# A pooled-attention and gated-MLP kernel: the second batch's attention product head by head in whole fp32 numbers

## The chip, the core and the metric

The kernel runs on one core of one Trainium2 chip. The metric is the device time of one execution in microseconds (us). Before the change the median of three runs is 535.81 us (535.55 to 536.28).

Names used below: PE is the matrix engine (PEld its weight loads, which have a row of their own in the trace), DVE the vector engine, ACT the scalar engine, POOL the general engine, SP the engine that only issues DMAs. PSUM is the memory that PE writes to, SBUF the working memory of all engines.

## What is computed

Eight batches, eight heads, 576 positions, head size 64. Keys and values are averaged over groups of 8 positions (so 72 pooled positions), softmax attention runs against them, the heads are laid side by side (512 columns), and a gated MLP with a mixing matrix over positions follows.

```python
k_p = k.reshape(B, H, 72, 8, D).mean(axis=3);  v_p = v.reshape(B, H, 72, 8, D).mean(axis=3)
scores = q @ k_p^T / sqrt(D);  e = exp(scores - max);  attn = e / (sum(e) + 1e-9)
x = (attn @ v_p), heads side by side                       # [8, 576, 512]
h = gelu(x @ w_in);  u, v = h[..., :512], h[..., 512:]
v_n = (v - mean) / sqrt(var + 1e-6) * g_ln
gated = u * (einsum('ts,bsd->btd', w_sg, v_n) + b_sg)
out = x + gated @ w_out
```

## The kernel before

All arithmetic must hold fp32 accuracy. Most matrix products therefore work on numbers split into a high and a low part in the format fp32r: for x = hi + lo and w = hi + lo the kernel issues three products (hi·hi, hi·lo, lo·hi). A product of whole fp32 numbers is one instruction in the program, and in the trace it stands as two matmuls, each with its own weight load.

The work is cut into steps, named by a letter, an index and a batch: `V1+2` is step V, index 1, batch 2. One list, `ORDER`, written out as a table of such names, says in which order the steps (each a generator that yields between its parts) are issued. All engines work through their instructions strictly in that order, so the table sets both what PE does next and what stands ahead of what on DVE, ACT, POOL and SP. A second table, `OTHER`, says for many small operations (copies, casts, subtractions) which of two engines does them.

The steps that the change and the prediction touch:

- D: filler matmuls on an identity matrix, 2 of whole fp32 numbers each; the program has 12 such steps.
- A, B, C, E: loads of keys, values, queries and of the values' last rows ("left"); `lv0`, `v1` and the like load and split the weights `w_in`, `w_sg`, `w_out`.
- K, S: pooled keys; scores of a pair of heads (a "group", 4 per batch), 5 fp32 matmuls with 144 columns each, then maximum, exponential, sum, the guard 1e-9, reciprocal and the product into `e`.
- P: pooled values. From batch 1 on, P2 puts the two heads of each group block by block into a 128 x 128 matrix, split into `vbh` and `vbl`. A group has 2 x 72 = 144 pooled rows, 16 more than the array has rows, so the 16 left over go into a second matrix `vl`.
- T: `e` is turned by 32 x 32 transposes on DVE and a trip through DRAM (`tfar`), loaded as `al` and split into `ah` (cast on ACT) and `al` (difference on DVE). L does the same for the 16 left-over rows of all groups (`lfar`, `lt`).
- V: the attention product. For each half of 288 positions it is four fp32r matmuls into the same 128 PSUM rows: `vbh·ah`, `vbl·ah`, `vl·lt`, `vbh·al`. The result x is copied and split (`x32`, `xhl`).
- H (and J for batch 0), U, W, O, Z: the MLP. H4 works on the last 64 positions and has matmuls with 64 weight columns between such with 128. O multiplies the gated values `ghi`, `glo` by `w_out`; Z stores.

Batch 0 takes another way through V: two products of whole fp32 numbers for each half (`vb·ah`, `vl·lt`), both over all 128 columns. `aps` and `mps` are the two pairs of PSUM tiles: attention uses the first, the MLP the second.

Of the kernel before, what the change touches and what calls it, by code (L numbers as in the profile page):

```python
# [31 lines left out]
V2+0 u1 u0 u0 s3 ls1 V0+0 s2 s0 J1+0 u2 u2 u2 T3+0 V3+0 V2+0 V2+0 u3 s4 s4 u2 A1+1 u3 o0 J1+0 K1+1 V3+0 o0 K1+1 J2+0
H0+0 lo1 B0+1 V3+0 B1+1 u3 u3 K0+1 s0 P0+1 s2 J2+0 J3+0 J3+0 H1+0 H0+0 o1 o0 V1+0 C2+1 V3+0 H0+0 V2+0 H2+0 D0+0 H1+0
H3+0 H2+0 S0+1 o0 o2 H0+0 H4+0 H1+0 H1+0 H1+0 C1+1 S1+1 S0+1 H0+0 H1+0 o1 H0+0 H3+0 S1+1 S1+1 S2+1 H4+0 S0+1 S2+1
S2+1 o2 U0+0 U0+0 H4+0 H4+0 s1 o1 o1 H2+0 S3+1 H2+0 o2 P1+1 U1+0 U2+0 H3+0 A0+2 U1+0 S0+1 o3 H4+0 H2+0 A1+2 K0+2 o3
H3+0 C0+2 U2+0 o2 T0+1 S0+1 H4+0 H2+0 S3+1 H3+0 T0+1 H4+0 H3+0 H4+0 U3+0 C3+2 o3 B0+2 S1+1 S1+1 S2+1 K0+2 S2+1 U3+0
o3 C1+2 W0+0 W1+0 W0+0 S3+1 S3+1 S3+1 S0+2 L0+1 T1+1 W0+0 W0+0 T0+1 L0+1 S0+2 P2+1 W1+0 P2+1 P2+1 P2+1 K1+2 W2+0
T0+1 S1+2 S0+2 L0+1 W2+0 S0+2 W1+0 W3+0 L0+1 V0+1 W3+0 C2+2 W2+0 T1+1 W1+0 T2+1 W3+0 W2+0 O0+0 V0+1 S0+2 K1+2 S1+2
O1+0 T1+1 T1+1 V1+1 S1+2 W3+0 B1+2 S1+2 L0+1 S2+2 V1+1 O0+0 O1+0 T2+1 V1+1 C0+3 P0+2 T2+1 T3+1 O0+0 S2+2 O2+0 T2+1
O1+0 E0+2 V2+1 T3+1 S2+2 T0+2 A0+3 O2+0 V1+1 V0+1 O2+0 Z2+0 T1+2 S2+2 V2+1 V2+1 O3+0 V0+1 O3+0 S2+2 T3+1 S3+2 T3+1  # L40
V3+1 S1+2 C1+3 O3+0 Z3+0 S3+2 V3+1 V3+1 K0+3 S3+2 H0+1 B0+3 V3+1 T0+2 H0+1 S3+2 H1+1 H0+1 H1+1 K0+3 S3+2 H2+1 H2+1
H0+1 H0+1 L0+2 H1+1 H1+1 H0+1 H3+1 H3+1 S0+3 H1+1 H3+1 T0+2 V2+1 H4+1 U0+1 H1+1 P1+2 H4+1 C0+4 P2+2 P2+2 H2+1 L0+2
L0+2 H4+1 U0+1 L0+2 P2+2 P2+2 U1+1 U1+1 S1+3 U2+1 H4+1 P2+2 S0+3 H2+1 H4+1 H2+1 L0+2 Z1+0 Z0+0 A1+3 H3+1 H3+1 H2+1
T0+2 V0+2 U3+1 K1+3 P0+3 H3+1 U2+1 H4+1 H4+1 U3+1 T1+2 C2+3 T2+2 S0+3 T3+2 H4+1 S1+3 W0+1 W0+1 K1+3 W1+1 T1+2 T1+2
V0+2 V1+2 W0+1 S0+3 W1+1 W1+1 W1+1 B1+3 T2+2 V1+2 S1+3 S1+3 V1+2 T2+2 S2+3 S2+3 T2+2 W2+1 W3+1 C3+3 V2+2 T3+2 W2+1
W2+1 S3+3 W2+1 W0+1 O0+1 V0+2 A0+4 T0+3 W3+1 W3+1 W3+1 O1+1 V2+2 C1+4 T1+3 V2+2 O0+1 E0+3 T3+2 T3+2 S2+3 V3+2 O0+1
# [36 lines left out]
""".split()


OTHER = set("""
G10 G11 G12 G13 H00 H10 H12 H13 H21 H22 H23 V00 V01 V02 V03 V13 V21 V22 V23 V33 W01 W10 W13 W21 W22 W23 X00 X03 X21
X22 X23 X30 X31 X32 X33 c10 c11 c21 e00 e01 e10 e11 e12 e20 e21 e22 e30 e31 e32 e33 g00 g04 g10 g11 g22 g24 h00 h02
h20 k10 k11 k20 k21 k31 l2 m00 m02 m03 m10 m11 m12 m21 m23 m30 m31 m32 m33 n00 n02 n03 n10 n11 n20 n21 n23 n30 n31
n32 n33 o0d o0h o1h o2d o3h p10 p11 p21 p30 s2 s2d s3 s3d s4d u0d u1d u2d u2h u3d u3h v0h v1h v2d v2h v3d x00 x01  # L90
x02 x22 z10 z20 z21 z30 z32 z33 z34
""".split())
# [765 lines left out]
```

## Time and profile before

| | before |
|---|---|
| median of the runs | 535.81 us (535.55 to 536.28) |
| profiled execution | 535.39 us, of which span 533.6 us |
| PE busy | 526.6 us, 99%, 3600 matmuls |
| weight loads busy | 498.8 us, 93% |
| DVE / ACT / POOL busy | 391.0 / 273.9 / 247.3 us (73 / 51 / 46%) |
| granted PE clock | 1.0 of full speed in every slice |
| chain that ended last | 94% PE |

How to read it: matmuls overlap in the record (one is entered with some 295 ns while the next begins 132 ns later), so what a matmul costs is read from the distance between starts, not from its own duration. A block of matmuls stands in the timeline as one row with its start, its length up to the end of the last one, and its count. "Idle before" a row is the time in which the engine had nothing running, with the instruction that released it.

### The profile page before, as it was taken

To read this page: it belongs to the slowest core of one execution; us is meant where nothing else is said; L and a number is where in the kernel's file an instruction comes from. 1 tells how busy PE (TensorE), PEld (TensorE's weight loads), DVE (VectorE), ACT (ScalarE), POOL (GpSimd) and SP (SyncE) were. 2 spreads that over 40 slices of the span, in tenths; PEclk is the share of its full clock that TensorE was granted. 3 is DMA by queue.
4 is the path that set the end of the run, shared out by engine and by line. 5 is a ranking of instruction groups with operands and counts; after the bars stand their busy time and mean duration, and the time that the engine had idled before them with its cause. 6 is when DMAs were issued, how large, how long until landed. Compare 5 with 4: busy or idle time off the path is not lost.

```text
span 533.6 us, 9547 instructions
## 1 busy us (share of the span) xinstructions
PE 526.6 (99%) x3600; PEld 498.8 (93%) x3600; DVE 391.0 (73%) x599; ACT 273.9 (51%) x521; POOL 247.3 (46%) x347
## 2 busy tenths in 40 slices
...
GB/s 282 398 332 172 68 146 117 192 208 112 135 139 155 154 114 201 71 109 157 91 152 78 60 174 180 88 58 166 106 137 3 83 117 68 23 1 1 90 1 89
DMA packets 42654, 67.08 MB, mean 126 GB/s; under 512 B 5232, under 2 KB 21616, under 8 KB 42608
## 3 DMA queue, kind: packets, MB, share of 16 engines
...
q10 hardware_dynamic: 288, 0.44, 0.2%
...
## 4 chain that ended last, share of the span: by engine, by line
PE 94%; DVE 2%; ACT 2%; POOL 1%; issue 0%; SPq 0%; DMA 0%; ACTq 0%; POOLq 0%
PE mps L140 79%; PE aps L140 15%; PE aps L186 1%; DVE nmax L506 1%; SPq L240 0%; DMA y<-lfar 0%; DVE glo L230 0%; POOL e L458 0%; ACT lt L559 0%; ACT raw L284 0%; POOL rstd L482 0%; ACT vg L662 0%; DVE e L463 0%; DVE mps L716 0%; ACT vg L491 0%
## 5 line engine op out<-in xcount | busy, mean ns | idle before, releaser
L140 PE MATMUL mps<-xhl,wih 128*128 128x288 f32 x512 | 88.8, 295 | 0.2 <-ACT vg L662 0.2
L140 PE MATMUL mps<-wih,xhl 128*128 128x512 f32 x256 | 81.2, 397 | 0.0
L140 PEld LDWEIGHTS mps<-xhl,wih 128*128 128x128 f32 x512 | 75.1, 188 | 1.0 <-ACT vg L662 0.4
L458 POOL TENSOR_TENSOR e<-e,ssum 128x720 f32<-128x720 f32 x28 | 41.4, 1481 | 62.6 <-DVE ssum L457 55.5
L140 PEld LDWEIGHTS mps<-wih,xhl 128*128 128x128 f32 x256 | 48.0, 188 | 10.9
L140 PE MATMUL mps<-wsh,vhh 128*128 128x288 f32 x256 | 55.2, 297 | 0.0
L140 PE MATMUL mps<-wsl,vhh 128*128 128x288 f32 x256 | 54.7, 295 | 0.0
L140 PE MATMUL mps<-wsh,vhl 128*128 128x288 f32 x256 | 54.6, 294 | 0.0
L140 PE MATMUL mps<-xhl,wil 128*128 128x288 f32 x256 | 54.5, 294 | 0.0
L140 PE MATMUL mps<-glo,woh 128*128 128x288 f32 x244 | 52.7, 295 | 0.8 <-DVE glo L230 0.8
L481 POOL TENSOR_TENSOR rstd<-mv,eps 128x1 f32<-128x1 f32 (+1 forms) x40 | 11.7, 293 | 89.4 <-DVE mv L667 89.3
L140 PE MATMUL mps<-ghi,woh 128*128 128x288 f32 x244 | 53.1, 297 | 0.1
L140 PE MATMUL mps<-ghi,wol 128*128 128x288 f32 x244 | 52.3, 295 | 0.0
L140 PE MATMUL mps<-wil,xhl 128*128 128x512 f32 x128 | 48.9, 397 | 0.0
L716 DVE SCALAR_TENSOR_TENSOR mps<-mps,both 128x576 f32<-128x576 f32 x32 | 26.2, 818 | 25.1 <-PE mps L140 25.0
L237 POOL TENSOR_TENSOR xhl<-x,xhl 128x576 fp32r<-128x576 f32 x19 | 27.3, 1440 | 36.4 <-ACT x L221 36.4
L221 ACT CAST xhl<-aps 128x576 fp32r<-128x576 f32 x29 | 18.6, 643 | 48.2 <-PE aps L140 45.7
L754 DVE TENSOR_TENSOR x<-mps,x 128x576 f32<-128x576 f32 x30 | 22.5, 750 | 26.7 <-PE mps L140 26.7
L140 PE MATMUL aps<-kbd,qT 128*128 128x144 f32 x300 | 41.4, 286 | 0.0
L140 PEld LDWEIGHTS mps<-wsh,vhl 128*128 128x128 f32 x256 | 41.1, 188 | 0.0
L140 PEld LDWEIGHTS mps<-xhl,wil 128*128 128x128 f32 x256 | 41.1, 187 | 0.0
L140 PEld LDWEIGHTS mps<-wsh,vhh 128*128 128x128 f32 x256 | 41.0, 188 | 0.0
...
## 6 DMA issues: line engine op xcount, KB each, us to landing
...
```

The costliest lines, as they stand in the source:

```text
L140: nc.tensor.matmul(o, lhsT, rhs, start=start, stop=stop)
L186: nc.tensor.transpose(ps[:rows, i * P:(i + 1) * P], src(i), ident if i < NT - 1 else swap)
L221: nc.scalar.copy(o, i)
L237: nc.gpsimd.tensor_tensor(lo, x, hi, op=ALU.subtract)
L458: (nc.gpsimd if key in OTHER else nc.vector).tensor_tensor(e, e, rec.unsqueeze(3).broadcast_to([P, NT, 2, SP]), op=ALU.mult)
L481: nc.gpsimd.tensor_tensor(rstd, var, eps[:n, 1:2], op=ALU.add)
L506: nc.vector.tensor_reduce(out=nmax, in_=every.rearrange("p s (h k) -> p s h k", h=2), axis=AX.X, op=ALU.max, negate=True)
L716: nc.vector.scalar_tensor_tensor(vs, vs, gcol[:, d:d + 1], bbc.rearrange("p (a n) -> p a n", a=2), op0=ALU.mult, op1=ALU.add)
L754: nc.vector.tensor_tensor(x, ps[:, :, 0:HALF], x, op=ALU.add)
```

## The change

For batch 1 alone (`BY_HEAD = (1,)`) the attention product is done head by head in whole fp32 numbers. The second head's 72 value rows are copied by DMA into a tile `vo` that begins at partition 0 (56 rows from `vp`, 16 from the left-over sums). T loads the turned `e` three times: 72 rows of head 0 into `ah`, 56 rows of head 1 and its 16 left-over rows into `al` (groups 1 and 3 use the tiles `lt0` and `lt1`). V has, for each half, one fp32 product per head: 72 rows by 64 columns, head 0 into PSUM rows 0 to 63, head 1 into rows 64 to 127. Nothing is split before the product: the casts and differences of T and L, and `vbh`, `vbl` and `vl` of P, are gone for this batch. The factor 1/8 of the pooled mean goes into the guard (sum times 8).

`ORDER` and `OTHER` are new tables for the whole program.

```diff
+BY_HEAD = (1,)
 ORDER = """
-A0+0 D0+0 D0+0 D0+0 D0+0 E0+0 D0+0 K0+0 C0+0 D0+0 E0+1 P2+1 D0+0 K0+0 S0+0 C1+0 lv0 D0+0 v1 D0+0 S0+0 v1 v1 S0+0
+A0+0 D0+0 D0+0 C0+0 D0+0 E0+0 D0+0 D0+0 K0+0 K0+0 lv0 v1 v0 v1 v1 S0+0 C1+0 v0 v0 S0+0 S1+0 S1+0 S0+0 S0+0 D0+0 D0+0
...
@@ step_P
+        if b in BY_HEAD:
+            vp = st["vp", b]
+            odd = st["vo", b] = per.tile([SP, G, D], F32, name="vo", tag="vl")
+            load(odd[0:P - SP], vp[SP:P])
+            for g in range(G):
+                load(odd[P - SP:SP, g], vlp[NL * g:NL * (g + 1), 0])
+            return
@@ guard
+        if b in BY_HEAD:
+            if key in OTHER:
+                nc.vector.scalar_tensor_tensor(ssum, ssum, float(POOL), eps[:, 2:3].unsqueeze(2).broadcast_to([P, NT, 2]),
+                                               op0=ALU.mult, op1=ALU.add)
+            else:
+                nc.vector.tensor_scalar(beside(flat), ssum, 1e-9, float(POOL), op0=ALU.add, op1=ALU.mult)
+            return
@@ step_L
-        far = afar(el, "lfar")
+        far = st["lfar", b] = afar(el, "lfar")
         yield
+        if b in BY_HEAD:
+            return
@@ step_T
+        if b in BY_HEAD:
+            ah, al = st["a", b, g] = [per.tile([SP, S], F32, name=t, tag=t) for t in (("ah", "al"), ("lt0", "lt1"))[g % 2]]
+            load(ah, far[0:SP])
+            load(al[0:P - SP], far[SP:P])
+            load(al[P - SP:SP], st["lfar", b][NL * g:NL * (g + 1)])
+            return
@@ step_V
+            if b in BY_HEAD:
+                for h, (w, x) in enumerate(((st["vp", b][0:SP, g], ah), (st["vo", b][:, g], al))):
+                    mm(o[D * h:D * h + D], w, x[:, sl], True, True)
+                continue
```

Three places of the order follow. First PE, the attention product of batch 1. Before, a group has these four products twice, once for each half, and the rows ahead of them are the end of step W:

```order
L140 MATMUL mps<-wth,vht 128x288 x2
L140 MATMUL mps<-wtl,vht 128x288 x2
L140 MATMUL aps<-ah,vbh 128x288
L140 MATMUL aps<-ah,vbl 128x288
L140 MATMUL aps<-lt,vl 128x288
L140 MATMUL aps<-al,vbh 128x288
```

Now, on the same engine, the products of groups 0 and 1 stand one behind the other (`vp` is head 0, `vo` head 1, 64x288 is the output of one head), behind the first products of step O:

```order
L141 MATMUL mps<-glo,woh 128x288 x2
L141 MATMUL aps<-ah,vp 64x288
L141 MATMUL aps<-al,vo 64x288
L141 MATMUL aps<-ah,vp 64x288
L141 MATMUL aps<-al,vo 64x288
L141 MATMUL aps<-lt_1006,vp 64x288
L141 MATMUL aps<-lt_1007,vo 64x288
```

The four groups stand in two blocks of 8 products, each product two matmuls in the trace; before they were four blocks of 8 matmuls. Ahead of the first block now stand 48 matmuls of step O (two output blocks whole); before, the first attention product of batch 1 came straight behind step W.

Second, the start of the program on DVE and SP. Before, DVE (whose `nmax` is the maximum of the first scores, and `top` a step of splitting `w_in`) and SP:

```order
L171 TENSOR_REDUCE mask<-pick 64x2
L506 TENSOR_REDUCE nmax<-mps 128x10
L463 TENSOR_TENSOR e<-mps,nmax 128x720
L283 TENSOR_SCALAR top<-top 128x512
```

```order
L240 DMA kraw<-in_k 128x1024
L240 DMA raw_139<-in_kv 128x512
L240 DMA left<-in_vleft 64x512
L240 DMA qT<-in_q 128x576
L240 DMA raw<-in_moe_w_in 128x2x1024
```

Now, the same two engines:

```order
L173 TENSOR_REDUCE mask<-pick 64x2
L285 TENSOR_SCALAR top<-top 128x512 x2
L523 TENSOR_REDUCE nmax<-mps 128x10
L480 TENSOR_TENSOR e<-mps,nmax 128x720
```

```order
L242 DMA kraw<-in_k 128x1024
L242 DMA raw_139<-in_kv 128x512
L242 DMA raw<-in_moe_w_in 128x2x1024
L242 DMA qT<-in_q 128x576 x3
```

On SP the first part of `w_in` moved from fifth to third place; on DVE two of its splitting operations now stand ahead of the first maximum, which waits for them. On ACT and POOL the matching steps of the two parts stand ahead of the first exponential and of the first product into `e` as well.

Third, filler matmuls on PE. Before, behind step J of batch 0 (`ident` is the filler, `kbd` the scores of batch 1, `xta` step H4):

```order
L140 MATMUL mps<-wil,xhl 128x512 x4
L140 MATMUL aps<-ident 128x128 x2
L140 MATMUL aps<-kbd_101,qT 128x144 x5
L140 MATMUL mps<-wih,xta 128x512
```

Now at the same place, and then behind step H4 of batch 2:

```order
L141 MATMUL mps<-wil,xhl 128x512 x4
L141 MATMUL aps<-ident 128x128 x4
L141 MATMUL aps<-kbd_102,qT 128x144 x5
L141 MATMUL mps<-wih,xta 128x512
```

```order
L141 MATMUL mps<-wih,xta 128x512
L141 MATMUL aps<-ident 128x128 x2
L141 MATMUL aps<-kbd_100,qT 128x144 x10
L141 MATMUL mps<-xhl,wih 128x288 x4
```

Of the 24 filler products 22 stood ahead of the first transposed `e` before, and 18 do now; two more stand at the first place shown, two at the second. The scores (products with `kbd`) stand in 30 separate blocks before and in 27 now.

## Rows read from the trace of the kernel before

**Rows 1.** The page, part 1: engine, busy us, share of the span, instructions.
```profile
PE 526.6 (99%) x3600; PEld 498.8 (93%) x3600; DVE 391.0 (73%) x599; ACT 273.9 (51%) x521; POOL 247.3 (46%) x347
```

**Rows 2.** Waits of PE, whole span: us in total, times, longest us.
```profile
PE aps L140 <- POOL ident masks.py:199: 1.4, 1, 1.4
PE mps L140 <- DVE glo L230: 0.8, 1, 0.8
PE aps L186 <- POOL e L458: 0.7, 1, 0.7
PE aps L140 <- ACT ah L221: 0.3, 1, 0.3
PE mps L140 <- ACT vg L662: 0.2, 1, 0.2
PE aps L140 <- ACT lt L221: 0.2, 1, 0.2
```

**Rows 3.** Timeline of PE, V of batch 1 group 1, then S, O: start, us, what.
```profile
93.30 0.29 PE L140 MATMUL aps<-ah,vbh 128*128 128x288 f32 x1
...
94.37 1.39 PE L140 MATMUL aps<-kbd,qT 128*128 128x144 f32 x10
95.50 0.52 PE L140 MATMUL mps<-ghi,woh 128*128 128x288 f32 x2
95.86 0.42 PE L140 MATMUL mps<-ghi,wol 128*128 128x288 f32 x2
96.12 0.43 PE L140 MATMUL mps<-glo,woh 128*128 128x288 f32 x2
```

**Rows 4.** Timeline of PE, V of batch 0 group 1, whole fp32 numbers.
```profile
30.07 0.65 PE L140 MATMUL aps<-lt,vl 128*128 128x288 f32 x2
30.55 0.65 PE L140 MATMUL aps<-ah,vb 128*128 128x288 f32 x2
```

**Rows 5.** Timeline of PE, step J (first row) and H4 of batch 0.
```profile
45.47 2.03 PE L140 MATMUL mps<-wih,xhl 128*128 128x512 f32 x8
...
51.42 0.39 PE L140 MATMUL mps<-wih,xta 128*128 128x512 f32 x1
51.65 0.40 PE L140 MATMUL mps<-wil,xta 128*64 128x512 f32 x1
51.88 0.39 PE L140 MATMUL mps<-wih,xta 128*128 128x512 f32 x1
```

**Rows 6.** Windows, tile al alone: stretch, length, busy PE, PEld, DVE, ACT.
```profile
60.00:110.00 50.00, 2.37 (x8) 1.53 (x8) 3.01 (x4) 2.70 (x4) 1.00 0.56 164
```

**Rows 7.** Timeline of SP, the start: DMA issues.
```profile
1.70 0.55 SPq L240 DMA_DIRECT2D left<-in_vleft  x1
...
2.91 0.44 SPq L240 DMA_DIRECT2D raw<-in_moe_w_in  x1
```

**Rows 8.** Timeline of ACT, first step of splitting w_in.
```profile
11.73 0.68 ACT L281 ACTIVATE top<-raw 128x512 f32<-128x512 f32 x1 [2.50 <-DMA raw<-in_moe_w_in]
```

**Rows 9.** Timeline of DVE, the first maximum.
```profile
10.83 0.91 DVE L506 TENSOR_REDUCE nmax<-mps 128x10 f32<-128x720 f32 x1 [7.02 <-PE mps L140]
...
12.60 0.42 DVE L283 TENSOR_SCALAR top<-top 128x512 int32<-128x512 int32 x1
```

**Rows 10.** Timeline of POOL, up to the first e.
```profile
13.15 1.30 POOL L286 TENSOR_TENSOR top<-top,raw 128x512 int32<-128x512 int32 x1 [2.85 <-DVE top L283]
14.51 0.61 POOL L225 CAST wih<-top 128x512 fp32r<-128x512 f32 x1
15.54 1.39 POOL L458 TENSOR_TENSOR e<-e,ssum 128x720 f32<-128x720 f32 x1 [0.42 <-DVE ssum L457]
```

**Rows 11.** Timeline of PE, the first turned e, and a filler block.
```profile
16.99 0.66 PE L186 MATMUL aps<-ident,e 128*128 128x128 f32 x4 [0.74 <-POOL e L458]
...
48.27 0.60 PE L140 MATMUL aps<-ident 128*128 128x128 f32 x4
48.71 1.39 PE L140 MATMUL aps<-kbd,qT 128*128 128x144 f32 x10
```

More of the change, by code (lines that the diff above doesn't have):

```diff
@@ L32 @@
[L32 to L46, printed above, removed]
@@ L82 @@
-Z3+7
+A0+0 D0+0 D0+0 C0+0 D0+0 E0+0 D0+0 D0+0 K0+0 K0+0 lv0 v1 v0 v1 v1 S0+0 C1+0 v0 v0 S0+0 S1+0 S1+0 S0+0 S0+0 D0+0 D0+0
+C2+0 C3+0 S0+0 S1+0 S1+0 D0+0 D0+0 v1 A1+0 K1+0 lv1 S1+0 v0 T0+0 K1+0 T0+0 v3 v2 S3+0 v3 v3 B0+0 B1+0 A1+1 v2 S2+0
+S2+0 S3+0 v2 S2+0 C0+1 P0+0 K1+1 L0+0 P1+0 S3+0 S2+0 L0+0 v3 ls0 P1+0 P0+0 S3+0 T1+0 S2+0 s2 V0+0 lu0 C1+1 lu1 s0 s1
+S3+0 T1+0 E0+1 V1+0 A0+1 lo0 H0+0 V0+0 V0+0 s0 v2 u1 u1 V1+0 V1+0 u0 L1+0 L1+0 s1 B1+1 J0+0 u0 T2+0 C2+1 K0+1 J0+0
+T3+0 V1+0 P2+1 u1 u1 H1+0 T2+0 V2+0 s3 s3 u3 u3 u0 V2+0 V2+0 T3+0 K0+1 J1+0 V3+0 u0 u2 P1+1 S0+1 u2 B0+1 J1+0 K1+1
@@ new lines @@
+u3 u3 V3+0 S0+1 o1 S1+1 o1 S0+1 u2 P0+1 S1+1 s2 S0+1 H2+0 J2+0 C3+1 J2+0 V3+0 J3+0 A0+2 S1+1 o1 J3+0 H0+0 S1+1 u2
+H3+0 S0+1 V2+0 H3+0 H1+0 o1 V0+0 D0+0 D0+0 V3+0 H0+0 H3+0 H0+0 H0+0 H0+0 o0 o0 C1+2 S2+1 H3+0 H2+0 H3+0 ls1 H3+0
+H4+0 H1+0 K0+2 H4+0 C2+2 s4 H4+0 lo1 H1+0 o0 H2+0 S3+1 S2+1 o0 U0+0 U1+0 U0+0 H4+0 C0+2 H4+0 s4 H2+0 H1+0 o3 o3 U2+0
+o2 U1+0 o2 K0+2 H2+0 U2+0 P2+1 H4+0 U3+0 H1+0 H4+0 H4+0 o2 H2+0 W0+0 E0+2 U3+0 W1+0 S2+1 o2 o3 T0+1 S3+1 S3+1 S2+1
+W0+0 S3+1 A1+2 S2+1 W0+0 o3 S0+2 B0+2 W1+0 W2+0 T1+1 S1+1 S3+1 L0+1 T0+1 T1+1 S0+2 W2+0 W0+0 S1+2 C3+2 W2+0 S0+2
@@ new lines @@
+T2+1 W1+0 W2+0 W1+0 W3+0 O0+0 W3+0 W3+0 O1+0 S1+2 S1+2 W3+0 O1+0 T3+1 S0+2 S0+2 O0+0 V0+1 V1+1 O1+0 K1+2 O0+0 S1+2
+K1+2 O2+0 V1+1 V0+1 V0+1 P2+2 T2+1 O2+0 V1+1 T3+1 V2+1 V2+1 C1+3 V3+1 O2+0 O3+0 S2+2 B1+2 T0+2 P1+2 S1+2 V2+1 V3+1
+P0+2 V3+1 S2+2 S2+2 A1+3 S3+2 S3+2 S3+2 T0+2 A0+3 O3+0 O3+0 S3+2 Z0+0 Z3+0 V0+1 H0+1 H0+1 S2+2 S2+2 H1+1 H2+1 C0+3
+S3+2 L0+2 H0+1 V1+1 H1+1 H0+1 K0+3 H2+1 H1+1 H1+1 T1+2 H0+1 K0+3 V3+1 V2+1 H3+1 C2+3 H4+1 S0+3 H1+1 H0+1 T0+2 K1+3
+H1+1 H3+1 H3+1 H4+1 S1+3 P2+2 H4+1 B1+3 T2+2 L0+2 H4+1 B0+3 H4+1 H4+1 U0+1 U0+1 U1+1 U1+1 H2+1 H3+1 L0+2 S0+3 H2+1
@@ new lines @@
+Z1+0 U2+1 U3+1 S1+3 P2+2 P2+2 L0+2 P1+3 P0+3 H3+1 H3+1 H2+1 P2+2 T0+2 Z2+0 V0+2 U2+1 T1+2 C0+4 K1+3 H2+1 U3+1 H4+1
+V0+2 S2+3 V0+2 V0+2 H4+1 C3+3 S0+3 T3+2 S0+3 W0+1 T1+2 W0+1 S0+3 W1+1 T1+2 W0+1 S1+3 V1+2 C1+4 S1+3 S2+3 W1+1 S1+3
+L0+2 E0+3 W2+1 T2+2 T2+2 V1+2 V1+2 W2+1 T2+2 V1+2 W3+1 V2+2 W0+1 W1+1 W1+1 W2+1 W2+1 A1+4 W3+1 W3+1 W3+1 O0+1 O0+1
+O0+1 S2+3 O1+1 O1+1 T3+2 T3+2 T3+2 A0+4 V2+2 V2+2 V2+2 S3+3 T0+3 V3+2 S2+3 O1+1 K0+4 Z0+1 O2+1 O2+1 V3+2 V3+2 S2+3
+K0+4 S3+3 V3+2 S3+3 O2+1 S3+3 S3+3 H0+2 H0+2 H1+2 H2+2 Z1+1 T0+3 K1+4 L0+3 H1+2 H0+2 O3+1 H2+2 O3+1 T1+3 H1+2 L0+3
@@ new lines @@
+H0+2 H2+2 C2+4 P2+3 P2+3 H0+2 H1+2 H3+2 H0+2 H3+2 O3+1 H4+2 Z3+1 D0+0 L0+3 H1+2 S0+4 H1+2 H3+2 L0+3 Z2+1 H4+2 H2+2
+T2+3 S1+4 H4+2 H4+2 P2+3 H2+2 U0+2 U1+2 S0+4 P2+3 P2+3 T0+3 T0+3 E0+4 V0+3 U0+2 U1+2 B1+4 S0+4 U2+2 U2+2 C3+4 U3+2
+H4+2 H4+2 H2+2 S1+4 T1+3 B0+4 T1+3 T1+3 H3+2 L0+3 H4+2 H3+2 C0+5 K1+4 V1+3 V1+3 H3+2 T2+3 P0+4 T3+3 H4+2 U3+2 P1+4
+W0+2 V0+3 W0+2 V0+3 V0+3 T2+3 S0+4 W1+2 T2+3 S0+4 S1+4 V2+3 W1+2 S2+4 S1+4 S2+4 S1+4 W1+2 A0+5 T3+3 C1+5 V2+3 W2+2
+W3+2 W2+2 T3+3 W0+2 W2+2 W0+2 T3+3 W3+2 S2+4 A1+5 V3+3 V3+3 V3+3 V2+3 V1+3 T0+4 H0+3 H0+3 H1+3 T1+4 H1+3 H0+3 H0+3
@@ new lines @@
+H0+3 K0+5 H1+3 W2+2 K0+5 W3+2 H1+3 S3+4 W1+2 W3+2 S2+4 H2+3 S3+4 O0+2 O0+2 P2+4 K1+5 H2+3 P2+4 O1+2 S3+4 O1+2 K1+5
+P2+4 S2+4 T0+4 T0+4 B0+5 P0+5 O0+2 Z0+2 T2+4 A0+6 V2+3 T0+4 S3+4 S3+4 O1+2 O2+2 H0+3 S0+5 O2+2 O2+2 H3+3 H3+3 S1+5
+H2+3 H2+3 L0+4 S0+5 L0+4 C0+6 S0+5 H3+3 O3+2 H3+3 H1+3 V1+3 O3+2 H3+3 O3+2 C3+5 P2+4 P2+4 Z2+2 H1+3 V3+3 H4+3 H4+3
+H4+3 E0+5 L0+4 U0+3 L0+4 U0+3 V0+4 S0+5 H3+3 U1+3 U2+3 U1+3 T1+4 T1+4 H4+3 K0+6 S1+5 C2+5 S1+5 H2+3 P2+5 U2+3 U3+3
+T1+4 B1+5 Z3+2 Z1+2 C1+6 L0+4 U3+3 H4+3 V1+4 H4+3 H4+3 V1+4 H2+3 T2+4 H4+3 V0+4 T0+5 W0+3 T2+4 V1+4 V1+4 W0+3 T3+4
@@ new lines @@
+T2+4 W0+3 W0+3 W1+3 S1+5 V2+4 T3+4 W1+3 S0+5 V0+4 P1+5 W2+3 W2+3 S2+5 S2+5 V2+4 V2+4 V2+4 W2+3 W2+3 V0+4 W3+3 T3+4
+T3+4 V3+4 W3+3 P2+5 P2+5 V3+4 V3+4 V3+4 W1+3 T0+5 S3+5 S3+5 S2+5 S2+5 H0+4 T1+5 H1+4 H0+4 W3+3 K0+6 S0+6 H1+4 H2+4
+H2+4 S2+5 H0+4 H0+4 H0+4 W1+3 A1+6 S3+5 P2+5 T2+5 S1+5 S0+6 W3+3 O0+3 H2+4 O0+3 H1+4 S3+5 S3+5 O0+3 O1+3 O1+3 Z0+3
+H0+4 S1+6 L0+5 P2+5 C2+6 O1+3 B0+6 H3+4 H3+4 H1+4 H3+4 O2+3 S1+6 L0+5 O2+3 O2+3 P0+6 T0+5 Z2+3 S0+6 T0+5 H1+4 H1+4
+H4+4 H4+4 O3+3 Z1+3 H4+4 H4+4 O3+3 S0+6 S1+6 C1+7 A0+7 C3+6 O3+3 H3+4 H3+4 H2+4 K1+6 K1+6 L0+5 U0+4 U1+4 U0+4 L0+5
@@ new lines @@
+S2+6 S0+6 B1+6 C0+7 P1+6 U1+4 H2+4 H2+4 E0+6 H4+4 H3+4 V0+5 Z3+3 U2+4 U3+4 T1+5 U2+4 T3+5 S2+6 H4+4 T1+5 T1+5 H4+4
+V1+5 U3+4 H4+4 L0+5 S1+6 V0+5 T2+5 W0+4 A1+7 T0+6 S2+6 W0+4 W0+4 W1+4 V0+5 V0+5 T2+5 T2+5 V2+5 W1+4 V1+5 V1+5 T3+5
+S2+6 S3+6 S3+6 K0+7 T3+5 T3+5 V2+5 V2+5 B0+7 V2+5 S3+6 W2+4 W2+4 W3+4 S3+6 V3+5 W3+4 V3+5 S2+6 P2+6 V3+5 H0+5 H0+5
+T0+6 W1+4 W1+4 K0+7 H1+5 H1+5 W0+4 S0+7 W3+4 S1+6 H0+5 W2+4 H0+5 H0+5 T0+6 T1+6 V3+5 H2+5 H1+5 W2+4 H2+5 S0+7 W3+4
+O0+4 T0+6 H1+5 H2+5 O0+4 O1+4 T2+6 O1+4 V1+5 P2+6 H1+5 O0+4 H1+5 S1+7 S0+7 O2+4 P2+6 O1+4 Z1+4 H2+5 O2+4 O2+4 H3+5
@@ new lines @@
+Z0+4 Z2+4 H2+5 H0+5 K1+7 P0+7 B1+7 S3+6 L0+6 L0+6 P2+6 P2+6 H4+5 H3+5 H4+5 H3+5 H4+5 S0+7 U0+5 U0+5 H3+5 U1+5 U1+5
+H3+5 L0+6 O3+4 C3+7 C2+7 L0+6 O3+4 H2+5 V0+6 S1+7 T1+6 O3+4 Z3+4 S1+7 S1+7 H4+5 U2+5 U3+5 K1+7 T1+6 U2+5 H4+5 T1+6
+V1+6 T0+7 L0+6 H4+5 T2+6 H4+5 U3+5 T2+6 H4+5 H3+5 W0+5 W0+5 V0+6 V0+6 T3+6 T2+6 V1+6 W1+5 W2+5 W1+5 W1+5 V1+6 V1+6
+V2+6 P1+7 E0+7 P2+7 S2+7 S2+7 W3+5 W2+5 V2+6 W0+5 S3+7 W0+5 S2+7 S0+7 T3+6 T3+6 T3+6 W3+5 W3+5 V2+6 V3+6 V3+6 V3+6
+W2+5 W2+5 H0+6 H0+6 S2+7 H1+6 W1+5 H1+6 S3+7 S2+7 S1+7 S3+7 H2+6 H0+6 H0+6 H2+6 O0+5 H1+6 W3+5 P2+7 O0+5 O0+5 V3+6
@@ new lines @@
+O1+5 S3+7 S3+7 O1+5 V0+6 T0+7 T1+7 H2+6 O2+5 L0+7 Z0+5 O1+5 T0+7 V2+6 O2+5 H1+6 H1+6 H1+6 O2+5 H0+6 Z2+5 H2+6 H3+6
+P2+7 P2+7 H0+6 P2+7 L0+7 H3+6 H4+6 U0+6 Z1+5 H4+6 H3+6 H4+6 H3+6 L0+7 L0+7 H4+6 L0+7 H3+6 U0+6 U1+6 T0+7 V0+7 U1+6
+T3+7 H3+6 U2+6 U2+6 U3+6 T1+7 O3+5 O3+5 H4+6 H2+6 U3+6 T2+7 H4+6 T1+7 T1+7 V1+7 H2+6 O3+5 H4+6 T2+7 T2+7 H4+6 Z3+5
+W0+6 V0+7 T2+7 V0+7 W0+6 W0+6 W0+6 W1+6 V1+7 V0+7 W1+6 V2+7 W2+6 T3+7 T3+7 W2+6 T3+7 V1+7 W2+6 W2+6 W3+6 W3+6 V2+7
+V3+7 V2+7 V3+7 V3+7 H0+7 H1+7 H0+7 H1+7 H0+7 W1+6 W1+6 O0+6 V2+7 H0+7 W3+6 W3+6 H0+7 H0+7 O0+6 O0+6 H1+7 H1+7 H1+7
```

61 lines of the change are left out of this document (14 added, 47 removed).

## The prediction, made before the changed kernel ran

> **What bounds the kernel now.** I read the busy shares first: PE is busy 526.6 us of a span of 533.6, DVE 73%, ACT and POOL less [rows 1]. The reader is to see that only PE can set the end. A busy share can hide gaps, since matmuls overlap in the record, so the waits of PE come next: six of them in the whole run, 1.4 us for the identity matrix at the start, then 0.7 for the first `e`, 0.3 and 0.2 in the first attention products, 0.2 before step U of batch 0 and 0.8 before step O of batch 0 [rows 2]. After the 1.4 that is 2.2 us. The time is therefore the sum of what PE is given to do, plus the chain that leads to the first `e` at 16.99 us [rows 11], plus these 2.2 us and a short tail. Work taken off DVE, ACT and POOL counts only as far as it shortens one of those waits. The last view is the timeline of the first 17 us, where PE runs filler and other engines set the pace.
>
> **The attention product itself.** Before, a group of batch 1 takes 94.37 - 93.30 = 1.07 us of PE [rows 3], four groups 4.28. A change between these operand formats costs about 0.10: the first pair after the scores lasts 95.86 - 95.50 = 0.36 where the next lasts 96.12 - 95.86 = 0.26 [rows 3].
>
> Now a group has four products of whole fp32 numbers. Such a product with 288 columns takes two matmuls and 30.55 - 30.07 = 0.48 us, so 0.24 for a matmul [rows 4]. No row shows two products in different columns of the array, so I bound the price from both sides. If nothing runs side by side, a group costs 4 x 0.48 = 1.94 (0.485 unrounded) and all four 7.76 us. If the heads overlap perfectly, half of that, 3.88. Between them lies a staggered case. Matmuls start in program order, and the two of one head write the same columns, so the second must wait for the first to stream through. It then runs beside the first matmul of the other head. A block of 16 matmuls then takes 9 slots, not 8: 9 x 0.24 = 2.18, two blocks 4.37. I take this one, although [rows 4] are nearest in form to the serial case: their products accumulate into the same 128 columns, and could not have overlapped whatever the array can do. With 0.10 for entering and for leaving each block, 0.4 less the 0.2 or so that entering and leaving cost before: 4.37 + 0.2 - 4.28 = +0.3 us. The ends are -0.4 and +3.7.
>
> In H4, matmuls with 64 weight columns stand between such with 128, and both steps take 0.23 us (51.42 to 51.65 to 51.88), while eight alike in step J last 2.03 altogether, 0.23 for each after the first one's 0.39 [rows 5]. A change of the width used costs nothing there, and I add nothing for it. The Trainium skill (TensorEngine Tiling (Array Packing), Key Properties) speaks against this change: switching the tiling mode drains the engine. By the page the two blocks would add four drains, for which it gives no figure; the trace shows none.
>
> That two column groups run at once no row here shows. The Trainium skill (TensorE: Matmul & The Clock Gate, Part 3) says that small outputs in distinct column groups run concurrently and that matmuls keep program order at start and end. By it the staggered price holds; without it, the serial one.
>
> **What is taken off the other engines.** In batch 1 the casts and differences for `al` and `ah` go, 2.70 us of ACT and 3.01 of DVE between 60 and 110 us [rows 6], and with them the same for `lt`, `vbh`, `vbl` and `vl`. All of it ran beside PE, so in the sum it is worth the 0.8 us wait for `glo` ahead of step O, for which DVE was late [rows 2]. That wait should go: DVE has less to do ahead of it. Step O moved ahead of V, so its `glo` is wanted about 1 us earlier after W, which is why I count no more than the 0.8 and not the whole relief. The extra DMAs (three loads of the turned `e` for a group in place of one, five copies into `vo`, none of the six `lfar` copies) lie beside 48 matmuls of step O at 0.13 each (a pair in 0.26 [rows 3]), 6.3 us: -0.8, with ends 0 and -1.
>
> **The start of the program, reordered.** The first part of `w_in` is issued in third place, where `left` stood: 1.70 instead of 2.91, so 1.2 us earlier [rows 7]. Its landing released ACT at 11.73 [rows 8]; I put it at 10.5. Two of its parts are now converted on ACT (0.68 each, to 11.9) and shifted on DVE (0.42 for the last, to 12.3) before the first maximum, which stood at 10.83 [rows 8, 9]: 1.47 later. One such shift stood in the chain behind the maximum and no longer does, -0.42 [rows 9]. POOL now has two sums and casts, 2 x (1.30 + 0.61) = 3.8 us, ahead of the first `e` [rows 10]; begun at about 12.6 it is free at 16.4, and `e` would be wanted at 15.54 + 1.05 = 16.6, so POOL is just not the last. The first turned `e` moves from 16.99 [rows 11] to about 18.0: +1.0. Ends: 0 if `w_in` lands before 9.5, +2.2 if it still lands at 11.7. Behind it PE has the same work up to the second attention product of batch 0, and what waited there for ACT, 0.3 and 0.2 [rows 2], has had the later start to catch up: -0.5, ends 0 and -0.5.
>
> **Fillers and format changes.** A block of four filler matmuls takes 48.71 - 48.27 = 0.44 us [rows 11]. Early ones fill time in which PE has nothing else; two blocks' worth now stand after J of batch 0 and in batch 2, where PE is short of time: +0.9, ends 0 (if they cover waits) and +0.9. The scores stand in 27 blocks instead of 30, 3 x 0.10 = -0.3. The 0.2 before step U [rows 2] I count as gone, since the filler there is longer.
>
> **Sum.** +0.3 (product) - 0.8 (wait before O) + 1.0 (start) - 0.5 (waits behind it) + 0.9 (filler) - 0.3 (format changes) - 0.2 (wait before U) = +0.4. Against the profiled execution's 535.39 that is 535.8. The median of the runs, 535.81, lies 0.42 above that execution, which would make 536.2. I give 536.0, in effect no change: 0.2% of this time is 1.07 us, and less than that a measurement of this kernel can't tell from nothing.
>
> **Rivals.**
> 1. The heads do not overlap: the column groups run one behind the other. Place: the two V blocks of batch 1. Price: 7.76 in place of 4.37, +3.4, which gives 539.4, slower. For it: fp32 matmuls in [rows 4] run strictly one behind the other, and nothing in this trace shows two at once. Against: those share their columns. It decides from a block of about 2.7 us on (2.18 and half of the 1.07 that a measurement can tell); without overlap a block takes 3.9.
> 2. The start is not late, and the filler covers waits: `w_in` lands early enough to hide behind the wait for the first keys and queries (-1.0), and the 0.9 of filler falls into time that PE would lose anyway. Then 534.1, faster. For it: ACT sat idle 2.50 us before the first conversion, and DVE 7.02 before its first maximum [rows 8, 9], so work can be done there for nothing. Against: [rows 8] show that ACT waited for just this load.
> 3. The relief does nothing because the new order puts another wait before O or W: +0.8, 536.8. This lies in the range of the forecast.
>
> **How the numbers follow.** The forecast and its near relative (3) have 0.41 together, with a range of their own from 535.0 to 537.0; rival 1 has 0.36, rival 2 has 0.23. Nearly all of the first is within 0.2% (535.81 ± 1.07), some 0.02 of it above. So faster 0.23, within 0.2% 0.39, slower 0.38. Rival 2 reaches down to about 533.9, rival 1 with its own start of ± 0.5 up to 539.6; the range 534.0 to 539.5 leaves out about 2 in 10.
>
> **What would show it.** In the profile after: two blocks of 16 matmuls for batch 1's V, 2.2 to 2.4 us each (right), or 3.9 (rival 1), and whether the matmul of the second head starts before the first head's second is through. The first turned `e` at 18 us or at 17. The wait of PE for `glo` gone. The filler in batch 2 with no idle time beside it. What would make the forecast wrong above all is a V block of 3.9 us.

## The result, and the profile after

The changed kernel takes 539.31 us (median of four executions, 539.18 to 540.10); the kernel before took 535.68 in the same comparison. The ratio is 1.0069, 95% interval 1.0051 to 1.0086: some 3.6 us slower, well outside the 0.2% that can be told from no change. The profiled execution took 539.42, with a span of 537.1.

Busy time is read first, as in [rows 1]: part 1 of the page after.

```profile
PE 527.5 (98%) x3600; PEld 496.0 (92%) x3600; DVE 382.2 (71%) x581; ACT 279.1 (52%) x541; POOL 261.6 (49%) x363
```

PE has 0.9 us more to do in the record, and the span is 3.5 longer. So PE stands idle longer. Its waits over the whole span, to set beside [rows 2] (us in total, times, longest):

```profile
PE aps L141 <- POOL ident masks.py:199: 1.4, 1, 1.4
PE aps L141 <- DVE e L475: 1.1, 1, 1.1
PE mps L141 <- issue: 0.8, 1, 0.8
PE aps L188 <- POOL e L475: 0.8, 1, 0.8
PE aps L141 <- ACT ah L223: 0.7, 2, 0.4
PE aps L141 <- DVE al L607: 0.4, 1, 0.4
PE mps L141 <- DVE vhl L232: 0.4, 1, 0.4
PE mps L141 <- ACT vg L691: 0.3, 1, 0.3
```

The wait for `glo` is gone. New are 1.1 for `e`, 0.8 for the issue, 0.4 for `al`, 0.4 for `vhl`, and `ah` is waited for twice. None of these lies in V of batch 1. Its first block on the timeline of PE, for [rows 3]:

```profile
94.89 0.43 PE L141 MATMUL mps<-glo,woh 128*128 128x288 f32 x2
95.25 0.46 PE L141 MATMUL aps<-ah,vp 72*64 72x288 f32 x1
95.25 0.46 PE L141 MATMUL aps<-al,vo 72*64 72x288 f32 x1
95.54 0.41 PE L141 MATMUL aps<-ah,vp 72*64 72x288 f32 x1
95.55 0.41 PE L141 MATMUL aps<-al,vo 72*64 72x288 f32 x1
...
97.34 0.53 PE L141 MATMUL mps<-ghi,woh 128*128 128x288 f32 x2
97.70 0.43 PE L141 MATMUL mps<-ghi,wol 128*128 128x288 f32 x2
```

The two heads start within 0.01 us of each other, and the next pair follows 0.24 after (0.29 for the first). The block lasts 97.34 - 95.25 = 2.09; the second one, from 100.70 to 102.80, 2.10. The matmul pairs on either side take 0.36 where 0.26 is usual (94.89 to 95.25, 97.34 to 97.70), so a block costs 2.09 + 0.10 + 0.10 = 2.29 in all, two of them 4.58.

Where PE loses its time shows when one subtracts, at a mark of the program, the PE work that stands in front of it from the time at which PE gets there (each matmul at its usual step, as 0.132 us for 288 columns, 0.234 for 512, 0.113 for scores; the whole run holds 519.2 us of it before and 518.8 after). What remains is the lag; it grows where PE waits. These are worked out from the whole timeline of PE; the last column is an experiment told below.

| mark | before | after | old order, own `vp` |
|---|---|---|---|
| first turned `e` (about 17 us) | 4.94 | 5.87 | 5.08 |
| last V of batch 0 (about 40) | 6.25 | 7.45 | 6.39 |
| first scores in W of batch 0 (about 77) | 7.40 | 10.44 | 7.50 |
| last V of batch 1 (about 106, 101) | 9.24 | 11.03 | 9.79 |
| first V of batch 2 (about 133) | 9.50 | 11.65 | 10.18 |
| second V of batch 2 (about 145) | 9.48 | 12.76 | 10.17 |
| last V of batch 7 | 11.06 | 14.92 | 11.74 |

After is 3.0 us behind at W of batch 0 already, gets 1.25 back by the last V of batch 1 (most of it the wait for `glo`), and then loses 0.4 up to the first V of batch 2, 1.1 at it and 0.6 later. The places, on the timeline of PE (start, us, what, idle before):

```profile
9.35 2.69 PE L141 MATMUL mps<-kbd,qT 128*128 128x144 f32 x20 [0.78 <-issue]
...
17.03 0.66 PE L188 MATMUL aps<-ident,e 128*128 128x128 f32 x4 [0.76 <-POOL e L475]
...
40.10 0.75 PE L141 MATMUL aps<-ah,vb 128*128 128x288 f32 x2 [0.38 <-ACT ah L223]
...
51.12 0.60 PE L141 MATMUL aps<-ident 128*128 128x128 f32 x4
52.80 0.68 PE L141 MATMUL aps<-ident 128*128 128x128 f32 x4 [1.07 <-DVE e L475]
...
58.13 0.79 PE L141 MATMUL mps<-xhl,wih 128*128 128x288 f32 x4 [0.33 <-ACT vg L691]
...
138.09 0.40 PE L141 MATMUL aps<-al,vbh 128*128 128x288 f32 x1 [0.43 <-DVE al L607]
...
185.16 0.61 PE L141 MATMUL aps<-ident 128*128 128x128 f32 x4
185.61 2.62 PE L141 MATMUL aps<-kbd,qT 128*128 128x144 f32 x20
```

The filler at 52.80 waits for a PSUM tile that DVE's normalisation of a batch 1 softmax still reads, and step U of batch 0 behind it waits for ACT all the same. Before, U began at 54.95. ACT ahead of U, first in the kernel before (its first `vg`, which had to wait for PE), then in the kernel after:

```profile
48.00 0.60 ACT L662 ACTIVATE vg<-mps 128x512 f32<-128x512 f32 x1 [1.06 <-PE mps L140]
```

```profile
45.87 0.32 ACT L489 ACTIVATE e<-aps,nmax 128x72 f32<-128x72 f32 x1
...
49.34 0.86 ACT L485 ACTIVATE e<-e 128x720 f32<-128x720 f32 x1
50.21 1.28 ACT L216 ACT_TABLE_LOAD   x1
...
51.62 0.58 ACT L691 ACTIVATE vg<-mps 128x512 f32<-128x512 f32 x1
...
56.78 0.81 ACT L508 ACTIVATE vg<-vg,mv,rstd 128x512 f32<-128x512 f32 x1 [1.89 <-POOL mv L507]
57.50 0.57 ACT L691 ACTIVATE vg<-mps 128x512 f32<-128x512 f32 x1
```

Two softmaxes of batch 1 (ten exponentials from 45.87, one of 0.86) and the table load, which stood at 45.45 before, now keep ACT busy up to the first `vg`, and PE no longer sets when it starts. This `vg` goes through statistics on DVE, `rstd` and `mv` on POOL and ACT again before the fourth `vg` can free the PSUM tile that U wants.

### The profile page after: what moved, and what is told of

It reads as the page before. It is cut to its first block, busy times and chain, and to the rows that moved or that the text cites. A ratio compares the mean times of both kernels' runs of the same rounds, so it can differ in the third digit from the quotient of the medians.

```text
span 537.1 us, 9545 instructions
## 1 busy us (share of the span) xinstructions
PE 527.5 (98%) x3600; PEld 496.0 (92%) x3600; DVE 382.2 (71%) x581; ACT 279.1 (52%) x541; POOL 261.6 (49%) x363
## 4 chain that ended last, share of the span: by engine, by line
PE 76%; DVE 11%; ACT 5%; POOL 4%; DMA 2%; issue 2%; SPq 0%; ACTq 0%; POOLq 0%; DVEq 0%
PE mps L141 64%; PE aps L141 11%; DMA raw<-in_moe_w_in 1%; DVE nmax L523 1%; DVE kp L364 1%; DVE bst L695 1%; ACT vg L508 1%; DVE ssum L494 1%; DVE al L607 1%; POOL rstd L498 1%; ACT L216 1%; POOL rstd L499 1%; DVE e L480 1%; POOL top L288 1%; DVE vhl L232 1%
## 5 line engine op out<-in xcount | busy, mean ns | idle before, releaser
L232 POOL TENSOR_TENSOR glo<-u,ghi 128x576 fp32r<-128x576 f32 x22 | 33.3, 1516 | 43.3 <-ACT ghi L223 37.8
L239 POOL TENSOR_TENSOR xhl<-x,xhl 128x576 fp32r<-128x576 f32 x22 | 32.2, 1470 | 37.4 <-ACT x L223 32.5
L141 PEld LDWEIGHTS mps<-ghi,woh 128*128 128x128 f32 x244 | 39.7, 188 | 1.8 <-DVE ssum L494 0.4
```

The costliest lines, as they stand in the source:

```text
L141: nc.tensor.matmul(o, lhsT, rhs, start=start, stop=stop)
L232: (nc.vector if key in OTHER else nc.gpsimd).tensor_tensor(o, x, y, op=op)
L239: nc.gpsimd.tensor_tensor(lo, x, hi, op=ALU.subtract)
```

## The experiments

Theory: the product itself costs nothing, and the new order loses the time in new waits. Rival: the product, or the loads that feed it, costs it in some place where the order can't be blamed. All ratios are to the kernel before.

**The product in the old order.**
```
-ORDER, OTHER of after
+ORDER, OTHER of before, less the second "T0+1" (step L must come first)
```


> The kernel after with the order and the choice of engines of the kernel before: only the attention product of batch 1 (with its loads) is changed; one step T of batch 1 is issued after step L, whose result it now needs. Theory A (the new order costs the time, the product nothing): V of batch 1 takes 4 x 1.05 us in place of 4 x 1.07, and with less work on DVE some of the 0.8 us wait of PE for glo goes: 535.0 to 535.9 us. Theory B (the product, or the DMAs that feed it, cost the time somewhere else): 538.5 to 539.5.

Measured: 538.26 us, 1.0048 (1.0033 to 1.0062). Near theory B's number, but not for its reason: V and its loads bring no wait of PE, and yet 2.4 us went. The trace says where. POOL, then PE:

```profile
106.98 0.45 POOL L367 TENSOR_TENSOR vp<-vraw 128x128 f32<-128x128 f32 x1 [8.72 <-issue]
107.39 2.79 POOL L238 TENSOR_TENSOR xhl<-x,xhl 128x576 fp32r<-128x576 f32 x2
```
```profile
108.84 0.73 PE L140 MATMUL mps<-wih,xhl 128*128 128x512 f32 x2 [1.33 <-POOL xhl L238]
...
123.31 0.45 PE L140 MATMUL mps<-wil,xta 128*64 128x512 f32 x1 [1.21 <-ACT xta L228]
```

POOL wants to write `vp` of batch 2. Before, `vp` was cast into `vbh` and `vbl` and free at once; by heads it is itself the weight, and is read by the last V of batch 1, whose last matmuls run from 106.44 to 106.85. POOL stands for 8.72 us, and the low halves of `xhl` behind it in its queue come late for H.

**The same, with a buffer for it.**
```
-st["vp", b] = per.tile([P, G, D], F32, name="vp")
+st["vo", b] = per.tile([P, 2, G, D], F32, name="vo", tag="vl")
+st["vp", b] = st["vo", b][:, 1]          # for b in BY_HEAD; vo itself is [0:SP, 0]
```


> As the run with the product alone (order of before), but vp of batch 1 lies in a buffer of its own, so that POOL's sum for vp of batch 2 need not wait until the last V of batch 1 has read it. Theory A (in the run with the product alone, POOL stood 8.72 us, up to 106.98, for that buffer, and PE's waits of 1.3 for xhl and 1.2 for xta behind it are all that the change cost there): both waits gone, 2.5 to 3.2 us less, 535.0 to 535.8, no more than before. Theory B (POOL waits there for something else, as the DMAs of the new loads): 538 again.

Measured: 535.76 us, 0.9999 (0.9990 to 1.0008), equal to before, as theory A had it. POOL writes `vp` at 98.55 without a wait, and behind the one for `ident` PE's waits are these:

```profile
PE aps L187 <- POOL e L478: 0.7, 1, 0.7
PE aps L140 <- ACT ah L222: 0.3, 1, 0.3
PE aps L140 <- DVE e L478: 0.2, 1, 0.2
PE mps L140 <- ACT vg L694: 0.2, 1, 0.2
PE aps L140 <- ACT lt L222: 0.2, 1, 0.2
```

So the held buffer was what the product cost in the old order on balance, and with that mended it gains nothing either: the 0.8 for `glo` is gone, and four separate V groups pay 0.35 each for going in and out (next but one). Between this kernel and after lie only the order, the choice of engines and the place of `vp`: 535.76 against 539.31. The place of `vp` costs nothing in after: the next `vp` is written once the last V of batch 1 (its last matmul ends at 102.87) has read the buffer, and neither DVE nor POOL (its part follows at 105.83) stands idle for it:

```profile
104.70 1.18 DVE L364 TENSOR_REDUCE vp<-vraw 128x128 f32<-128x1024 f32 x1
```

**Same columns.** A control on that kernel: 128 weight columns for either product of a pair, accumulated, in place of 64 each.
```
-mm(o[D * h:D * h + D], w[:, g], x[:, sl], True, True)
+mm(o, w[:, gg:gg + 2], x[:, sl], h == 0, h == 1)      # gg = min(g, G - 2)
```


> The run with vp in a buffer of its own (order of before), with the two products of a pair given 128 weight columns each (the values of two neighbouring groups, so V of batch 1 holds other numbers) and accumulated into the same rows of PSUM, in place of 64 columns each in a column group of its own: as many matmuls of as many columns of data. Theory A (what makes two of them run side by side is the column group): a V group takes 8 x 0.24 = 1.94 and the changes, some 2.1 us in place of 1.12, four groups +3.6 to +3.9: 539.0 to 539.7. Theory B (whole fp32 products of 72 rows overlap in any columns): 535.5 to 536.0.

Measured: 538.45 us, 1.0047 (1.0033 to 1.0060). Group 1 here, then in the kernel with a buffer for `vp`:

```profile
92.88 2.10 PE L140 MATMUL aps<-lt,vo 72*128 72x288 f32 x8
94.82 1.39 PE L140 MATMUL aps<-kbd,qT 128*128 128x144 f32 x10
```
```profile
92.50 1.19 PE L140 MATMUL aps<-lt,vo 72*64 72x288 f32 x8
93.62 0.64 PE L140 MATMUL aps<-kbd,qT 128*128 128x144 f32 x3
```

94.82 - 92.88 = 1.94, eight steps of 0.24 one behind the other, against 93.62 - 92.50 = 1.12: the column groups do run it in half the time. The total rose by 2.7, less than the 3.6 that theory A gave. In same columns the first group goes straight from and into its neighbours (no time lost at its edges), while by column groups the four steps at its edges are 0.10, 0.05, 0.10 and 0.10 longer. That makes 4 x (0.97 - 0.35) = 2.5.

**Head by head in the program.**
```
-for n in range(2): for h, (w, x) in heads: mm(...)
+for h, (w, x) in heads: for n in range(2): mm(...)
```


> The kernel after with the eight products of a V block of batch 1 issued head by head: of each group both column halves of head 0, then both of head 1, in place of one half of each in turn. Theory A (two products run side by side only where they stand next to each other in the program): per block 13 slots of 0.24 us in place of 8, 3.2 us in place of 2.09; two blocks +2.1, 541.4. Theory B (each column group works through its own list): blocks stay at 2.1, 539.3.

Measured: 539.10 us, 1.0059 (1.0046 to 1.0072), as after. Four matmuls of one head now stand ahead of the other's four, and they pair as before:

```profile
95.64 0.46 PE L141 MATMUL aps<-ah,vp 72*64 72x288 f32 x1
95.65 0.46 PE L141 MATMUL aps<-al,vo 72*64 72x288 f32 x1
```

**Fillers early.**
```
-... V0+0 D0+0 D0+0 V3+0 ... Z3+1 D0+0 L0+3 ...
+K0+0 K0+0 D0+0 ... v0 D0+0 D0+0 T0+0 ...
```


> The kernel after with its three late filler blocks (two after J of batch 0, one in batch 2) issued before 17 us, where PE waits 0.8 us for the issue and 0.8 for the first e anyway. Theory A (each late block costs its 0.44 us, and the one that waits for a PSUM tile 1.07 more): 2.0 to 2.5 us less than after, 536.8 to 537.3. Theory B (step U of batch 0 waits for ACT's vg at 58.13 whatever PE does before, so the two blocks and their wait lie beside that chain): only the block in batch 2 is saved, 538.7 to 539.1, and U still starts at about 58.1.

Measured: 538.92 us, 1.0059 (1.0045 to 1.0072). Theory B: only about 0.4 less than after, which these intervals don't separate from nothing. PE without the two blocks:

```profile
54.34 0.50 PE L140 MATMUL mps<-wih,xta 128*128 128x512 f32 x1 [1.09 <-ACT xta L228]
...
58.87 0.79 PE L140 MATMUL mps<-xhl,wih 128*128 128x288 f32 x4 [1.17 <-ACT vg L690]
```

In this execution the first turned `e` stood at 17.78, 0.75 later than in after. This arose ahead of the moved fillers: the eight key matmuls from 5.91 on lasted 1.97, in after 1.22. U begins 41.09 behind it, in after 41.10. The fillers and their wait of 1.07 lie beside the chain through ACT.

**Scores into the gap.**
```
-... S0+1 o1 S1+1 ... P0+1 S1+1 ... V0+0 D0+0 D0+0 V3+0 H0+0 H3+0 ...      # S1+1 four times ahead of V0+0
+... S0+1 o1 ... P0+1 ... V0+0 S1+1 V3+0 H0+0 H3+0 ... S1+1 ... W1+0 S1+1 ... S1+1 S2+1
+K0+0 K0+0 D0+0 ... v0 D0+0 T0+0                                           # and n11, e11 to OTHER
```


> The kernel after with the scores of group 1 of batch 1 moved from ahead of the last part of J of batch 0 to behind it, in the place of the two filler blocks there (which go to the start), and their softmax behind step U. Theory A (what the opening loses is PE work to lay beside the chain from J through vg, its statistics and vg to U, some 7 us long; two blocks of scores were spent too early, and fillers stand in for them): U of batch 0 starts 0.7 to 1.1 us earlier, 57.0 to 57.4, and the run takes 538.2 to 538.6. Theory B (that chain starts late for reasons of its own, as ACT's ten exponentials and the table load before vg): U starts at 58 still, 539.0 to 540.0.

Measured: 540.72 us, 1.0091 (1.0074 to 1.0107), above both theories and 1.4 above after, though the two intervals overlap. The chain did come sooner: the fourth `vg` at 56.13, 39.2 behind the first turned `e` where it was 40.5. But PE had lost it to another wait, for the PSUM tile of the next scores (DVE reads the scores before them until 57.00), and U began at 58.31:

```profile
57.10 1.46 PE L140 MATMUL aps<-kbd,qT 128*128 128x144 f32 x10 [2.15 <-issue]
```

**V of batch 2 behind the scores,** and this together with the last.
```
-... Z2+0 V0+2 U2+1 ... H4+1 V0+2 S2+3 V0+2 V0+2
+... Z2+0 U2+1 ... H4+1 S2+3 V0+2 V0+2 V0+2 V0+2
```


> The kernel after with the first V of batch 2 placed behind the next block of scores in place of ahead of it (1.13 us later). Theory A (that V waits for lt and al, 0.4 + 0.8 us late by the trace of after, and the chain that brings them does not hang on PE here): the wait goes, 0.9 to 1.1 us less than after, 538.2 to 538.4. Theory B (the wait moves on to the softmax or to step H of batch 2, which then come later): 539.0 to 539.6.

> The two edits to the order of after together: the first V of batch 2 behind a block of scores, and the scores of group 1 of batch 1 in the gap behind J. If both losses are separate they add: 537.2 to 537.8. If the order has further waits of the same kind behind these, less: 538 to 539.

Measured: 543.67 us, 1.0142 (1.0124 to 1.0161), and 545.46, 1.0184 (1.0166 to 1.0203), both above all that was expected. V itself no longer waits, but the scores took the other of two PSUM tiles, and the next V waits for DVE to have read them:

```profile
150.61 0.37 PE L140 MATMUL aps<-ah,vbh 128*128 128x288 f32 x1 [3.21 <-DVE e L479]
...
152.20 0.69 PE L140 MATMUL mps<-wsl,vhh 128*128 128x288 f32 x2
```

The wait of 3.21 isn't the whole loss. Behind it PE ran from 151.7 to 155.2 at a granted clock of 0.51 (1.2 GHz), so that a matmul of 288 columns took 0.24 in place of 0.132 (the second row). I estimate from these steps that this cost another 1.6 us. Three of the four executions of the first run had a mean granted clock of 0.996 or 0.997 and took 543.62 to 544.61; the fourth, at 1.0, took 541.93.

**DVE's queue ahead of `al`.**
```
-... S1+3 P2+2 ... T0+2 Z2+0
+... P2+2 ... T0+2 S1+3 Z2+0
```


> The kernel after with one token moved: the maximum and the difference of group 1 of batch 3 (1.8 us of DVE at 129.67 to 131.5) come behind al of the first V of batch 2 in DVE's queue. Theory A (that V waits because DVE works through its queue without a gap from 128 us to al at 137.17): al 1.2 to 1.8 us earlier, no wait at V, and 0.7 to 1.0 us less than after, 538.3 to 538.6. Theory B (lt or vl come from ACT and POOL no earlier): the wait stays, 539.2 to 539.6.

Measured: 540.59 us, 1.0085 (1.0071 to 1.0099), above theory B's number, but for its reason: DVE, given 1.8 us less to do, stands and waits for `lt` from ACT, and the next scores wait for ACT besides.

```profile
133.90 0.75 DVE L579 TENSOR_TENSOR lt<-y,lt 32x576 fp32r<-32x576 f32 x1 [1.65 <-ACT lt L577]
```

**Two orders spliced.** After's order to 71 us or to 108 us, then before's.
```
+ORDER = after[:k] + [x for x in before if not yet done]      # k at W0+0, at H0+1
```


> The order of the kernel after up to step W of batch 0 (some 71 us), then that of the kernel before, without what is done already; engine choices of batch 0 and of the weights from after, the others from before; product by heads. Theory A (most of the loss arises in the opening: 0.9 for fillers that now stand in busy time, 1.2 at the filler that waits for a PSUM tile, 1.1 in step J, less 0.5 ahead of it): 2.5 to 3.0 above the run with the product alone, 538 to 538.8. Theory B (the loss arises behind 71 us, in the stages of batch 1 and 2): within 0.8 of the run with the product alone.

> The order and the engine choices of the kernel after up to step H of batch 1 (some 108 us), then those of the kernel before, without what is done already; vp of batch 1 in a buffer of its own. Theory A (the loss arises in two places, about 1.5 us up to 108 us and 1.0 at the V of batch 2, with the rest in later stages): 1.2 to 2.0 above the run with the old order and vp in its own buffer, 537.0 to 537.8. Theory B (all of the loss lies behind 108 us): within 0.5 of that run, 535.3 to 536.3. If a seam between the orders adds waits of its own, the lag up to 108 us can still be read.

Measured: 557.89 us, 1.0409, and 553.22, 1.0330. Both failed as experiments: at the seam steps stand too close, as in the second, where PE waits

```profile
PE aps L140 <- DVE e L478: 7.7, 2, 7.2
```

behind 108 us. In both, PE also ran at a granted clock of 0.5 in two stretches (53.6 to 60.4 and 80.9 to 91.1 in the first, 113.7 to 120.5 and 147.8 to 151.2 in the second). Up to 108 us the second's lag repeats that of after (10.23 at the scores in W of batch 0), which tells nothing new.

**A better version.** With a buffer for `vp`, V of groups 2 and 3 one behind the other:
```
-V2+1 T3+1 S2+2 T0+2 A0+3 O2+0 ... V3+1
+T3+1 S2+2 T0+2 A0+3 O2+0 V2+1 V3+1 ...                   # and n22 to OTHER
```


> The run with vp in a buffer of its own (order of before), with V of groups 2 and 3 of batch 1 one behind the other, and with the normalisation of group 2 of batch 2 on POOL, so that it keeps no reciprocal in the PSUM tile that the next scores wait for. Theory A (a change between V and other matmuls costs 0.1 us, and the wait of PE for DVE's e there, 0.3, goes): 535.2 to 535.5 us, a little less than both kernels. Theory B (V of group 3 now waits for its PSUM tile, or H for the later V of group 2): 535.8 to 537.

Measured: 538.40 us, 1.0044 (1.0030 to 1.0058), above both theories. V of group 3 now comes before its load has landed:

```profile
PE aps L140 <- DMA lt<-tfar: 1.2, 1, 1.2
```

This is from the fastest of its five executions (537.57). In three of the others the mean granted clock was 0.997, and they took 538.40 to 538.99.

No version beat the kernel before.

## Why the prediction was right or wrong

The time lies just inside the range, but the forecast of no change was wrong: 536.0 is 3.3 us short. That it lies inside is luck. The range reaches so high only for rival 1, whose 539.4 is close to the measured 539.31 although its mechanism fell. Step by step:

- **Product, +0.3.** Right in size, 4.58 - 4.28, but by errors that cancel. No stagger: a block has 8 slots, not 9, which is 0.24 less for each of the two. Its edges cost 0.35, not 0.20. And V had no edges to pay before, where I allowed 0.2 in all (see the format changes below). Also wrong was that a change of the width used costs nothing; the control shows about 0.35 for going into column groups and out. Rival 1 fell: two products in same columns take 1.94 where column groups take 1.12. The rule that switching the tiling mode drains the engine (the Trainium skill, TensorEngine Tiling (Array Packing), Key Properties) fits these edges, 0.35 for a block, better than my reading of [rows 5] did.
- **`glo`, -0.8.** Right: gone. The tile `al` in the stretch of [rows 6] now has work on PE and PEld alone, DVE and ACT stand at 0:

```profile
60.00:110.00 50.00, 2.37 (x8) 0.93 (x8) 0.00 (x0) 0.00 (x0) 1.00 0.43 120
```

- **Start, +1.0.** Wrong. The first turned `e` is at 17.03, not 18.0; the other end of the bound held ("0 if `w_in` lands before 9.5"): ACT converts the first two parts from 9.36 on, not from 11.73 as in [rows 8]. DVE shifts them in time it had idle, as rival 2 had it, and its first maximum comes at 11.00 against 10.83 in [rows 9]:

```profile
9.36 1.26 ACT L283 ACTIVATE top<-raw 128x512 f32<-128x512 f32 x2
```
```profile
10.08 1.00 DVE L285 TENSOR_SCALAR top<-top 128x512 int32<-128x512 int32 x2 [6.25 <-ACT top L283]
11.00 0.90 DVE L523 TENSOR_REDUCE nmax<-mps 128x10 f32<-128x720 f32 x1
```

- **Fillers, +0.9.** Right in the ledger: the lag at the first turned `e` is 0.93 larger, since four filler products fewer fill the same 17 us. But moving them back bought only about 0.4, not clear of the noise; the block in batch 2, with no idle time beside it, would account for that. The two behind J lie beside the chain to U.
- **Format changes, -0.3.** Nothing, by a misreading of [rows 3]. The ten scores there last 1.39 us up to the end of the last one, and one alone lasts 0.29, so they are entered 0.122 apart and would want 1.22 together. The next pair is entered 1.13 after the first of them, 0.09 early, and the 0.10 that it then takes longer only makes this up. Three blocks of scores fewer save nothing by this.
- **Waits behind the start, -0.5, and before U, -0.2.** These are the steps that failed most. From the first turned `e` to W of batch 0 the lag grew by 10.44 - 5.87 = 4.57, before by 7.40 - 4.94 = 2.46: +2.1 where I had -0.7. I had asked only whether the old waits would shrink, and not what the new order lays into ACT's and DVE's queues ahead of `vg`.
- **Not in the sum:** by the table 0.4 on the way to the first V of batch 2, 1.1 at it, and 0.6 in later batches. My rival 3 was of this kind, but I looked for its wait at O and W of batch 0, and priced it at 0.8.

That the new order with its engine choices, and not the product, takes the 3.6 us is shown by the run with the old order and an own `vp`, together with the trace of after, where nothing waits for `vp`. That ACT's queue ahead of U is what costs the opening is read from the trace and borne out by the run without fillers. How the loss divides among the waits isn't settled: each of four repairs of one place left PE with a wait on another queue or PSUM tile, and none got more than the 0.4 back.
